# The last store of a scan-and-FFN kernel as two stores of 64 rows on two queues

## The chip, the cores and the metric

The kernel runs on one core of a Trainium2 chip. A core has five engines with their own instruction streams: TensorE (PE, matmuls, with its weight loads listed as PEld), VectorE (DVE), ScalarE (ACT), GpSimd (POOL) and SyncE (SP). SyncE does no arithmetic here; it issues almost all DMA transfers. A transfer is issued by an engine's instruction and then carried out by the core's 16 DMA engines; its landing is signalled by a semaphore. The metric is the device time of one execution in microseconds, as the median of several runs.

## The reference: what is computed

Input x has 2048 tokens of 512 numbers. It is normalised per token, and the normalised xn goes two ways that are multiplied at the end:

```python
xn = layernorm(x)
s  = 2 * Re(scan(xn) @ C.T) + xn * Dskip      # diagonal complex recurrence over the 2048 tokens, 512 states
g  = silu((gelu(xn @ w_gate) * (xn @ w_up)) @ w_down)      # 512 -> 1376 -> 512
out = x + s * g                                # bf16, 2048 x 512
```

## The kernel before

The 2048 tokens are worked on in four slabs (s = 0 to 3) of 512, each of four tiles (m = 0 to 3) of 128 tokens. For a slab the kernel normalises, turns the tokens by a transposing DMA, multiplies by gate and up weights (`gate_tile`, L436), turns the product (`at_t`, L463), multiplies by the down weights (`down_pair`, L471), and beside that runs the recurrence (`half`, L537), whose scans are on VectorE. The output of a tile is made in `y_part` (L488), called by `y_tile` (L515):

- ScalarE puts the skip term into a PSUM bank (L493), TensorE adds eight matmuls to it (L497);
- VectorE multiplies the bank by the gate g (L502) and adds x (L508) into an output buffer `ot[o]`;
- SyncE stores the buffer to `out` (L513), 128 rows, one row per token.

Tiles are 512 columns wide. The last tile of all (s = 3, m = 3) goes in two halves of 256 columns (`HD`), each with its own bank, multiply, add and store, so that the last store has 128 rows of 256 columns, 64 KB. For the tiles m = 0 and m = 1 of the last slab, `cuts` (L511) makes two stores of 256 columns out of the one buffer after its addition is done; all other stores are of 512 columns, 128 KB. The last two tiles use two buffers of their own, which the trace calls `junk`, so they wait for no earlier store.

Nothing is scheduled automatically. `Plan.add` collects steps with what they read and write, and `Plan.run` (L70) emits them in a list written out at the head of the file, `ORDER` (L21). Every engine executes its own instructions in the order in which they appear there. An instruction waits for the semaphores of what it reads; a DMA also waits until the transfer that used its semaphore before has landed. At the end of the program (L840 in the trace) SyncE waits for the transfers that are still out, and then all engines meet in a closing sequence.

ScalarE issues only three small DMAs, at the head of the kernel (L256, the parameters `pv`); all the others are on SyncE.

Of the kernel before, what the change touches and what calls it, by code (L numbers as in the profile page):

```python
# [17 lines left out]
PE, ACT, DVE, POOL, SP = "PE", "ACT", "DVE", "POOL", "SP"  # L18
# [26 lines left out]
)  # L45


# [33 lines left out]
def kernel(  # L81
# [17 lines left out]
    nc = tc.nc  # L99
    P = 128  # L100
    S = 2048
    D = 512
# [6 lines left out]
    NS = S // TS  # L109
    M = TS // P  # L110
# [4 lines left out]
    HD = D // 2  # L115
# [5 lines left out]
    V, A, G, T = nc.vector, nc.scalar, nc.gpsimd, nc.tensor  # L121
# [6 lines left out]
    def sb(name, shape, dt=BF16):  # L128
        return consts.tile(shape, dt, name=name)
# [30 lines left out]
    ot = [sb(f"ot{i}", [P, D]) for i in range(2)]  # L160
# [18 lines left out]
    def dve(n, emit, reads=(), writes=(), rate=1.0, base=DV, **kw):  # L179
        return pl.add(DVE, base + n / 960.0 / rate, emit, reads, writes, lag=0.13, **kw)  # L180

    def acts(n, emit, reads=(), writes=(), ptr=0, **kw):
        return pl.add(ACT, AC + 0.12 * ptr + n / 1200.0, emit, reads, writes, lag=0.16, **kw)

    def pe(n, cols, emit, reads=(), writes=(), **kw):
        return pl.add(PE, n * (cols + 6) / 2400.0, emit, reads, writes, lag=0.22, **kw)
# [4 lines left out]
    def dma(eng, issue, land, emit, reads=(), writes=(), **kw):  # L191
        return pl.add(eng, issue, emit, reads, writes, lag=land, **kw)
# [3 lines left out]
    out_td = out[0]  # L196
# [291 lines left out]
    def y_part(s, m, c0, c1, bank, key, seed, e):  # L488

        w = c1 - c0  # L490
        ps = bank[:, 0:w]
        if seed:
            acts(w, lambda: act(out=ps, in_=sk[s % 2][:, m, c0:c1], func=AF.Copy), [("sk", s % 2, m)], [key])  # L493

        def f():
            for j in range(2 * NPT):
                T.matmul(ps, lhsT=hst[s % 2][:, j // NPT, j % NPT, m * P : (m + 1) * P], rhs=C2[:, j // NPT, j % NPT, c0:c1],  # L497
                         start=(j == 0 and not seed), stop=(j == 2 * NPT - 1), skip_group_check=True)
        pe(2 * NPT, w, f, [("hst", s % 2, 0), ("hst", s % 2, 1)] + C2S + ([key] if seed else []), [key])
        gi, b = g2s[s, m]  # L500
        if seed:
            dve(w, lambda: V.tensor_tensor(out=yg[e][:, c0:c1], in0=ps, in1=g2[gi][:, b, c0:c1], op=ALU.mult), [key, ("g2", gi, b)], [("yg", e, c0)])  # L502
        else:
            ys = tF[:, 0, c0:c1]
            dve(w, lambda: V.tensor_tensor(out=ys, in0=ps, in1=sk[s % 2][:, m, c0:c1], op=ALU.add), [key, ("sk", s % 2, m)], [("tF",)])
            dve(w, lambda: V.tensor_tensor(out=yg[e][:, c0:c1], in0=ys, in1=g2[gi][:, b, c0:c1], op=ALU.mult), [("tF",), ("g2", gi, b)], [("yg", e, c0)])
        o = 2 + m % 2 if s == NS - 1 and m >= M - 2 else m % 2
        dve(w, lambda: V.tensor_tensor(out=ot[o][:, c0:c1], in0=yg[e][:, c0:c1], in1=x_tok[:, s * M + m, c0:c1], op=ALU.add),  # L508
            [("yg", e, c0), ("x", s, m)], [("ot", o, c0)], rate=2.0)
        mg = s * TS + m * P  # L510
        cuts = (0, HD) if (NS - 1, 0) <= (s, m) < (NS - 1, M - 2) else (c0,)  # L511
        for lo, hi in zip(cuts, (*cuts[1:], c1)):
            dma(SP, 0.35, 1.5, lambda lo=lo, hi=hi: nc.sync.dma_start(out=out_td[mg : mg + P, lo:hi], in_=ot[o][:, lo:hi]), [("ot", o, c0)], [("out", s, m, lo)], svc=(2, 0.4, 0.9))  # L513

    def y_tile(s, m):  # L515
        i = y_n[0] % 2
        seed = True
        y_n[0] += 1
        if (s, m) == (NS - 1, M - 1):
            for h in range(2):  # L520
                r, ps = bank()
                y_part(s, m, h * HD, (h + 1) * HD, ps, ("bank", r), True, m % 2)
        else:
            y_part(s, m, 0, D, ybank[i], ("y", i), seed, m % 2)
# [175 lines left out]
    c1, s1 = cbt[:, :, 1], sbt[:, :, 1]  # L700
# [32 lines left out]
    for pt in range(NPT):  # L733
# [3 lines left out]
            out=C2[:, 0, pt, :], in0=CT[:, 0, pt, :], scalar=cre[:, pt : pt + 1], in1=tF[:, 1, :], op0=ALU.mult, op1=ALU.subtract),  # L737
            ["coef", ("CT", 0), ("tF",)], [("C2", 0, pt)], base=0.13)
        dve(512, lambda pt=pt: V.scalar_tensor_tensor(
            out=C2[:, 1, pt, :], in0=CT[:, 1, pt, :], scalar=ncre[:, pt : pt + 1], in1=tF[:, 0, :], op0=ALU.mult, op1=ALU.subtract),  # L740
# [104 lines left out]
```

## Time and profile before

| | |
|---|---|
| median of 3 runs | 178.52 us (178.51 to 178.72) |
| span of the profiled execution, first to last instruction | 176.3 us |
| time around the span (median less span) | 2.2 us |
| PE busy | 172.3 us (98%) |
| DVE busy | 156.9 us (89%) |
| ACT busy | 123.5 us (70%) |
| last instruction that computes (DVE, L508) | starts at 173.60 us, takes 0.29 us |
| stores by SyncE | 19, of which 16 from `ot` and 3 from `junk` |

The profile is of one execution; its times are counted from the first instruction. The time of that execution as a run was not recorded apart from its span, so the span stands for it, with the 2.2 us around it. In the rows, "SPq" and "ACTq" are the instruction queues of SyncE and ScalarE that issue DMAs; the time of such a row is that of the issue, not of the transfer. "To landing" is from the issue to the last semaphore event of the transfer.

### The profile page before, as it was taken

What the parts mean: (1) busy time and instruction counts of PE and PEld (TensorE: products, weight loads), DVE (VectorE), ACT (ScalarE), POOL (GpSimd) and SP (SyncE); (2) the same over time, 40 slices, a digit from 0 to 9 for tenths busy, and PEclk for the clock granted to TensorE, in tenths of its full rate; (3) what the DMA queues carried; (4) which work ended last, traced back from release to release, by engine and by line L of the source; (5) the groups of instructions that cost most, each with busy time, mean ns of one, the idle gap of its engine ahead of it and who ended that gap; (6) DMA issues with size and microseconds to landing.
All of it is one profiled execution on the core that took longest, in us unless ns stands there. A gap on an engine that the chain in (4) does not pass through costs nothing.

```text
span 176.3 us, 2421 instructions
## 1 busy us (share of the span) xinstructions
PE 172.3 (98%) x847; PEld 82.3 (47%) x847; DVE 156.9 (89%) x252; ACT 123.5 (70%) x236; POOL 11.2 (6%) x25
## 2 busy tenths in 40 slices
PE   8999999999999999999999999999999999999992
PEld 2555454444454544444455454444444455444451
DVE  3859999999699984999979999899999999999764
ACT  6599979969999999799588845383058518482240
POOL 2660030000200000000040000000000000000000
PEclk9999999999999999999999999999999999999999
DMA  5999999998000809422000084194000007627112
GB/s 156 322 371 225 205 226 260 219 279 137 0 0 12 188 20 192 95 75 46 0 0 6 30 137 95 41 182 86 0 0 0 0 30 162 65 41 154 45 58 76
DMA packets 48355, 18.66 MB, mean 106 GB/s; under 512 B 40312, under 2 KB 47832, under 8 KB 48344
## 3 DMA queue, kind: packets, MB, share of 16 engines
q1 hardware_dynamic: 48320, 18.52, 48.8%
q8 instruction: 6, 0.10, 0.3%
q14 instruction: 5, 0.04, 0.1%
q10 hardware_dynamic: 24, 0.00, 0.0%
HBM read 6.46 MB, written 2.10 MB: 49 GB/s over the span
## 4 chain that ended last, share of the span: by engine, by line
PE 97%; DVE 1%; issue 0%; DVEq 0%
PE ring L449 32%; PE ring L481 22%; PE ring L547 16%; PE ybank L497 15%; PE ring L418 5%; PE ring L388 3%; PE ybank L418 2%; PE ring L299 1%; DVE yg L502 1%; PE ybank L299 1%; DVE junk L508 1%; PE ybank L328 0%; PE ring L303 0%; PE ring L313 0%; PE ring L603 0%
## 5 line engine op out<-in xcount | busy, mean ns | idle before, releaser
L449 PEld LDWEIGHTS <-xnT 128*128 128x128 bf16 x288 | 28.2, 98 | 28.4
L481 PE MATMUL ring<-wd,atT 128*128 128x512 bf16 (+1 forms) x176 | 39.3, 379 | 0.0
L449 PE MATMUL ring<-wg,xnT 128*128 128x512 bf16 (+1 forms) x144 | 31.6, 357 | 0.0
L449 PE MATMUL ring<-wu,xnT 128*128 128x512 bf16 (+1 forms) x144 | 31.3, 357 | 0.0
L547 PE MATMUL ring<-xnT,BT 128*128 128x512 bf16 x128 | 30.1, 379 | 0.0
L578 DVE TENSOR_TENSOR_SCAN Fs<-rho,ini,W 128x512 bf16<-128x512 f32 x24 | 29.7, 1271 | 0.1
L452 ACT ACTIVATE ub<-ring 128x512 bf16<-128x512 f32 (+1 forms) x36 | 19.2, 555 | 13.8 <-PE ring L449 13.7
L497 PE MATMUL ybank<-C,hst 128*128 128x512 bf16 x120 | 27.7, 379 | 0.0
L481 PEld LDWEIGHTS <-atT 128*128 128x128 bf16 (+1 forms) x176 | 17.2, 97 | 20.9
L549 ACT ACTIVATE U<-ring 128x512 bf16<-128x512 f32 x32 | 18.1, 599 | 7.5 <-PE ring L547 7.5
L452 ACT ACTIVATE gt<-ring 128x512 bf16<-128x512 f32 (+1 forms) x36 | 19.5, 556 | 3.7 <-PE ring L449 3.5
L497 PEld LDWEIGHTS <-hst 128*128 128x128 bf16 x136 | 13.3, 98 | 14.0
L484 ACT ACTIVATE g<-ring 128x512 f32<-128x512 f32 x16 | 9.4, 594 | 14.3 <-PE ring L481 14.2
L547 PEld LDWEIGHTS <-BT 128*128 128x128 bf16 x128 | 12.5, 97 | 14.8
L559 DVE TENSOR_TENSOR Q<-U,tab 128x4096 bf16<-128x4096 bf16 x8 | 18.3, 2289 | 0.9 <-ACT tab L646 0.7
L559 DVE TENSOR_TENSOR Q<-Fs,tab 128x4096 bf16<-128x4096 bf16 x8 | 18.3, 2288 | 0.1
L502 DVE TENSOR_TENSOR yg<-ybank,g 128x512 bf16<-128x512 f32 x15 | 10.2, 685 | 5.8 <-PE ybank L497 5.7
L763 ACT ACTIVATE junk<-x_tok 128x512 bf16<-128x512 bf16 x16 | 10.0, 632 | 1.2 <-DMA x_tok<-in_A_x_dram 1.2
L493 ACT ACTIVATE ybank<-sk 128x512 f32<-128x512 bf16 x15 | 9.1, 605 | 1.7 <-DVE yg L502 1.6
L768 ACT ACTIVATE xna<-x_tok,nb,rs 128x512 bf16<-128x512 bf16 x12 | 9.5, 812 | 0.0
L578 DVE TENSOR_TENSOR_SCAN Fs<-rho,W 128x512 bf16<-128x512 f32 x8 | 9.3, 1210 | 0.1
L458 DVE TENSOR_TENSOR at<-gt,ub 128x1024 bf16<-128x1024 bf16 x12 | 8.2, 683 | 0.0
(140 smaller groups left out, 169.7 us busy)
## 6 DMA issues: line engine op xcount, KB each, us to landing
x_tok<-in_A_x_dram SPq DMA_DIRECT2D x3, 512.0 KB, 4.6
out_dram<-ot SPq DMA_DIRECT2D x12, 128.0 KB, 1.8
wd<-in_B_w_down_dram SPq DMA_DIRECT2D x1, 1280.0 KB, 7.1
wu<-in_B_w_up_dram SPq DMA_DIRECT2D x4, 256.0 KB, 3.9
wg<-in_B_w_gate_dram SPq DMA_DIRECT2D x1, 864.0 KB
x_tok<-in_A_x_dram SPq DMA_DIRECT2D x4, 128.0 KB, 2.1
wg<-in_B_w_gate_dram SPq DMA_DIRECT2D x1, 512.0 KB, 6.0
wu<-in_B_w_up_dram SPq DMA_DIRECT2D x1, 352.0 KB, 5.3
```

Of the source, the lines that this page charges most:

```text
L418: T.matmul(ps[:, 0 : b - a], lhsT=lhs(k), rhs=wt[:, k, a:b], start=(k == 0), stop=(k == KT - 1))
L449: T.matmul(ps[:, 0 : b - a], lhsT=xnT[:, s % 2, m, k, :], rhs=wt[:, k, a:b], start=(k == 0), stop=(k == KT - 1))
L452: acts(b - a, lambda: act(out=dst[:, a:b], in_=ps[:, 0 : b - a], func=AF.Copy if up else AF.Gelu_apprx_tanh), [("bank", r)], [key], table= ...
L481: T.matmul(ps[:], lhsT=atT[:fs, k, m * P : (m + 1) * P], rhs=wd[:fs, k, :], start=(k == 0), stop=(k == NFT - 1))
L497: T.matmul(ps, lhsT=hst[s % 2][:, j // NPT, j % NPT, m * P : (m + 1) * P], rhs=C2[:, j // NPT, j % NPT, c0:c1], start=(j == 0 and not seed ...
L502: dve(w, lambda: V.tensor_tensor(out=yg[e][:, c0:c1], in0=ps, in1=g2[gi][:, b, c0:c1], op=ALU.mult), [key, ("g2", gi, b)], [("yg", e, c0)])
L547: T.matmul(ps[:], lhsT=BT[:, ri, k, pt * P : (pt + 1) * P], rhs=xnT[:, s % 2, :, k, :], start=(k == 0), stop=(k == KT - 1))
L549: acts(512, lambda q=q, ri=ri, ps=ps: act(out=U[ui][:, ri, q, :], in_=ps[:], func=AF.Copy), [("bank", r)], [("U", ui, q, ri)])
L559: dve(4096, lambda: V.tensor_tensor(out=Qf, in0=src.unsqueeze(1).to_broadcast(WQ), in1=table, op=ALU.mult), reads, ["Q"], rate=2.0)
L578: pl.add(DVE, 1.12 if s == 0 else 1.185, lambda ri=ri, q=q, pt=pt, first=first: V.tensor_tensor_scan(out=Fs[:, ri, q, :], data0=rho[:, pt ...
L763: acts(512, lambda i=i, fn=fn, sc=sc, m=m: act(out=junk()[:], in_=x_tok[:, s * M + m, :], func=fn, scale=sc, accum_out=sx[:, s, i, m : m + ...
L768: acts(512, lambda m=m: act(out=xn[m], in_=x_tok[:, s * M + m, :], func=AF.Identity, scale=rs[:, s, m : m + 1], bias=nb[:, s, m : m + 1]), ...
```

## The change

Two edits in `y_part`, and the list `ORDER` numbered anew for them. The second half of the last tile is stored by two DMAs of 64 rows each: rows 0 to 63 by SyncE, rows 64 to 127 by ScalarE. Both read the same buffer and wait for the same addition. And of the last slab only tile 0 is still stored in two halves of columns; tile 1 is stored whole. In `ORDER` the numbers shift by one for the step that falls away, and ScalarE's new DMA is step 671, the last step of ScalarE. On TensorE, VectorE and GpSimd the instructions and their order are the same in both kernels; SyncE has one store less in tile 1, and ScalarE one DMA more.

```diff
-    586, 639, 637, 640, 601, 641, 626, 635, 630, 616, 643, 646, 644, 651, 652, 638, 647, 657, 658, 642, 662, 663, 667, 668, 636, 631, 648, 653, 654,
-    659, 660, 664, 665, 669, 670, 649, 650, 655, 656, 661, 666, 671,
+    586, 639, 637, 640, 601, 641, 626, 635, 630, 616, 643, 646, 644, 651, 652, 638, 647, 656, 657, 642, 661, 662, 666, 667, 636, 631, 648, 653, 654,
+    658, 659, 663, 664, 668, 669, 671, 649, 650, 655, 660, 665, 670,
...
         mg = s * TS + m * P
-        cuts = (0, HD) if (NS - 1, 0) <= (s, m) < (NS - 1, M - 2) else (c0,)
+        if (s, m, c1) == (NS - 1, M - 1, D):
+            for eng, issue, p0 in ((SP, nc.sync, 0), (ACT, A, P // 2)):
+                dma(eng, 0.25, 1.4, lambda issue=issue, p0=p0: issue.dma_start(out=out_td[mg + p0 : mg + p0 + P // 2, c0:c1], in_=ot[o][p0 : p0 + P // 2, c0:c1]),
+                    [("ot", o, c0)], [("out", s, m, c0, p0)])
+            return
+        cuts = (0, HD) if (s, m) == (NS - 1, 0) else (c0,)
         for lo, hi in zip(cuts, (*cuts[1:], c1)):
             dma(SP, 0.35, 1.5, lambda lo=lo, hi=hi: nc.sync.dma_start(out=out_td[mg : mg + P, lo:hi], in_=ot[o][:, lo:hi]), [("ot", o, c0)], [("out", s, m, lo)], svc=(2, 0.4, 0.9))
```

## The prediction

> **What bounds the kernel now.** I read the chain of work that ended last first, then its tail in order of time, then what SyncE does behind it, then the transfers in the last two microseconds. On the page, the chain's shares by engine:
>
> ```profile
> PE 97%; DVE 1%; issue 0%; DVEq 0%
> ```
>
> TensorE carries 97% of the chain, and the change touches none of its instructions: the order of PE, VectorE (DVE) and GpSimd is the same in both kernels, and ScalarE (ACT) has one DMA more at its end. So only what stands behind the last matmul can move. The chain's end in order of time (start, length, what):
>
> ```profile
> 171.42 0.70 DVE yg L502
> ...
> 172.57 0.35 DVE yg L502
> ...
> 172.94 0.29 DVE junk L508
> 173.23 0.35 DVE yg L502
> ...
> 173.60 0.29 DVE junk L508
> ```
>
> The last instruction that computes ends at 173.60 + 0.29 = 173.89, but the page gives a span of 176.3. The remaining 2.4 us are the last store and the closing of the program, which the chain of work leaves out. The stores that SyncE issues in that stretch, one window of its timeline each:
>
> ```profile
> 170.80 0.33 SPq L513 DMA_DIRECT2D out_dram<-ot  x1
> 171.18 0.42 SPq L513 DMA_DIRECT2D out_dram<-ot  x1
> 172.59 0.33 SPq L513 DMA_DIRECT2D out_dram<-junk  x1
> 173.26 0.33 SPq L513 DMA_DIRECT2D out_dram<-junk  x1
> 173.91 0.33 SPq L513 DMA_DIRECT2D out_dram<-junk  x1
> ```
>
> The first two rows are the halves of tile 1 of the last slab, the third is tile 2 whole, the last two are the halves of tile 3. The very last store is issued at 173.91, 0.02 us after its addition ended. Next, what the DMA engines do from there on (one row for each stretch; the last two columns are their mean busy share and GB/s):
>
> ```profile
> 174.24:174.74 0.50, 0.00 (x0) 0.00 (x0) 0.00 (x0) 0.00 (x0) 0.00 (x0) 1.00 0.21 57
> 174.74:175.10 0.36, 0.00 (x0) 0.00 (x0) 0.00 (x0) 0.00 (x0) 0.00 (x0) 1.00 0.63 182
> 175.10:175.46 0.36, 0.00 (x0) 0.00 (x0) 0.00 (x0) 0.00 (x0) 0.00 (x0) 1.00 0.00 0
> 175.46:176.28 0.82, 0.00 (x0) 0.00 (x0) 0.00 (x0) 0.00 (x0) 0.00 (x0) 1.00 0.00 0
> ```
>
> The 64 KB of the last store move only in the second row, 0.36 us. Before it lie 0.33 us of issue and 0.50 us in which its packets have not begun (the 0.21 of the first row is the store before it); behind it 0.36 us with nothing on the engines before SyncE hears that the store landed. What SyncE waits for at the end, and when (waits from 172 on, longest first; then its closing waits at L840, by window):
>
> ```profile
> SPq L840 <- DMA out_dram<-junk: 0.9, 2, 0.6
> ...
> L840 SPq EVENT_SEMAPHORE  x3: 28/28/28, 174.4 to 174.5; - x3
> ...
> L840 SPq EVENT_SEMAPHORE  x2: 28/28/28, 174.5 to 174.8; - x2
> ...
> L840 SPq EVENT_SEMAPHORE  x1: 28/28/28, 175.5 to 175.5; - x1
> ```
>
> So the tail of before reads: addition ends 173.89; issue 173.91 to 174.24; first packets 174.74; last packets 175.10; landed and waited for at 175.46 (1.5 us after the issue); closing 0.82; end 176.28. This 1.55 us from the addition to the wait is all that the change can work on.
>
> I make the sum against that span. The median of the runs shown is 178.52, that is 2.2 us more than 176.3; those 2.2 us lie around the span, and I take them as unchanged.
>
> **Part 1: tile 1 of the last slab as one store.** Removed is one store instruction. Before, SyncE is done with the two halves at 171.18 + 0.42 = 171.60 and its next store can't go before the addition that ends at about 172.57 (its row is 172.59), so SyncE idles for 0.99 us. One whole store is issued in 0.33 at 170.80 (the 128 KB store at 172.59 took the same 0.33 as the 64 KB ones), so SyncE is free at 171.13 and waits longer for the same addition. Its landing (median time from issue to landing, by size):
>
> ```profile
> out_dram<-ot SPq DMA_DIRECT2D x12, 128.0 KB, 1.8
> ...
> out_dram<-ot SPq DMA_DIRECT2D x4, 64.0 KB, 1.6
> ...
> out_dram<-junk SPq DMA_DIRECT2D x2, 64.0 KB, 1.5
> ```
>
> At 1.8 it lands at 172.6 instead of 171.18 + 1.6 = 172.8. Nobody waits for either before SyncE's closing waits, which start at 174.3, and no later addition writes that buffer again. The next packets on the engines are those of the store at 172.59, whose own issue and lead of about 0.83 us put them at 173.4. Cost and gain: 0. The cover is the 0.99 us of idle SyncE; if it were gone, the second issue, 0.42, would count.
>
> **Part 2: the second half of tile 3 as two stores of 64 rows.** Both wait for the addition that ends at 173.89. SyncE's store sits where the old one sat. ScalarE's DMA stands behind its last activation and only the closing stands behind it; ScalarE is free long before: its last two instructions, from its timeline,
>
> ```profile
> 169.69 0.68 ACT L493 ACTIVATE ring<-sk 128x256 f32<-128x256 bf16 x2
> ```
>
> end at 170.37, so nothing of ScalarE is delayed, and the added wait has nobody behind it.
>
> Step by step, each against the old store:
>
> (a) SyncE's issue. The rows give 0.33 for 64 KB and for 128 KB of 128 rows, so bytes don't set it. No 64-row store is in the trace. The nearest with fewer rows are the three small loads at the head, four rows each, on ScalarE's queue:
>
> ```profile
> L256 ACTq DMA_DIRECT2D pv<-in_A_log_dt_dram x1: 554/554/554, 0.8 to 0.8; - x1
> L256 ACTq DMA_DIRECT2D pv<-in_A_Lambda_im_dram x1: 259/259/259, 1.4 to 1.4; - x1
> L256 ACTq DMA_DIRECT2D pv<-in_A_Lambda_re_dram x1: 314/314/314, 1.7 to 1.7; - x1
> ```
>
> Bounds: 0 to -0.07 (0.33 to 0.26). I take 0, since 64 rows are nearer to 128 than to 4 in what an engine gets. This is not yet a gain of the kernel, because ScalarE's half must land too.
>
> (b) ScalarE's issue. The same three rows: 0.26 to 0.55, against the old 0.33, so -0.07 to +0.22. The first, 0.55, came when this queue had issued nothing before and a table load was running on ScalarE; the later two took 0.26 and 0.31. At 173.9 the queue has been idle for 172 us, which speaks for the slow one; ScalarE is otherwise idle, which speaks for the fast ones. I take the middle row, 0.31, which is level with SyncE's 0.33: 0.
>
> (c) The packets. 64 KB in 0.36 us at a mean share of 0.63 over the core's 16 engines (the second of the four stretches): at least eleven of them take part in one store already. Two halves on the same engines are the same bytes; if they run side by side, the last packet ends when it ended before. If each half had its engines to itself, it would take half of 0.36, a gain of 0.18; if one half were started wholly behind the other, 0. A check by landing: 128 KB in 1.8, 64 KB in 1.5 to 1.6, so half the bytes would be worth 0.10 to 0.15 at most. Bounds 0 to -0.18; I take 0, since one store spreads over most engines now and the two halves overlap in time.
>
> The rule that speaks against this edit: the Trainium skill, "DMA: Bandwidth & Descriptors", section "Rules for kernel authors", says of two transfers to disjoint partition halves not to bother, since both spread over the same 16 engines, whichever engine issues them. By that rule (c) is 0; without it (c) would be up to -0.18. The trace agrees as far as it goes (share 0.63 as a mean over 16 engines with one store in flight), but no run yet shows two queues storing at once.
>
> (d) The closing. SyncE now waits for two last stores. In the rows above three closing waits that were due at once stand within 174.33 to 174.50, and each takes 28 ns: a pitch of about 0.06. If the half whose wait comes first in the list lands last, its partner's wait follows for 0.06 more; if it lands first, 0. I take 0.03.
>
> Sum: part 1 0, (a) 0, (b) 0, (c) 0, (d) +0.03: the span goes from 176.3 to 176.33, the time from 178.52 to 178.55. A measurement of this kernel can tell about 0.2%, that is 0.36 us, from no change; the forecast is that nothing can be told.
>
> **The rivals.**
>
> Rival 1, faster: the fixed parts shrink with the rows. If issue and the 0.50 us ahead of the first packet depend on how many rows a queue must describe, and the two queues do this side by side, then the issue falls by 0.07 (a), the packets by 0.18 (c), and some of the 0.50 goes as well; a quarter of it would be 0.13. Together -0.38, 178.14. For it: 0.83 of the 1.55 us lie before the first packet, and two engines would share that work. Against it: stores of 64 KB and 128 KB with the same 128 rows took the same 0.33, and a load of 4 rows still took 0.26, so nearly all of the issue stands whatever the rows. Half of this rival, -0.15 to -0.25, lies within 0.2%.
>
> Rival 2, slower: ScalarE's queue is cold. Place: ScalarE's one DMA at 173.9, the first on that queue since 1.7 us. Price: an issue like the first row, 0.55 instead of 0.33, +0.22; its wait comes after SyncE's half, +0.06; and a landing like the slower stores (1.6 where the last one takes 1.5), +0.10. Together +0.38, 178.90. It decides from the point where ScalarE's half lands later than 175.46, which is as soon as its issue takes longer than SyncE's with the same lead. For it: 172 us without a DMA on that queue. Against it: the 0.55 happened beside a table load and beside SyncE's first load, and its successors overlapped SyncE's issues at 0.26 and 0.31. With the issue alone, +0.22 or +0.28 with (d), the time would be 178.74 to 178.80, within 0.2%.
>
> Rival 3, the change doesn't do what it says: part 1 does nothing in any case (SyncE idles 0.99 us there), and part 2 leaves the same 1.5 us of issue, lead, packets and receipt, only twice. That is 178.52 and coincides with the forecast but for 0.03; it has no time of its own.
>
> **How the numbers follow.** Forecast with rival 3: 0.66, all within 0.2%. Rival 1: 0.16, of which 0.10 is faster by over 0.2% (below 178.16). Rival 2: 0.18, of which 0.14 is slower by over 0.2% (above 178.88; I give the full price most, because an idle queue can cost in its lead too, which no row bounds). So faster 0.10, within 0.2% 0.76, slower 0.14. The range: the unknown costs reach from -0.25 ((a) and (c)) to +0.38 (rival 2), which is 178.27 to 178.90; the runs of before lie between 178.51 and 178.72, and I add some 0.05 at either end for that, 178.20 to 178.95. Outside are left the full rival 1 and the worst of rival 2.
>
> **What would show it.** In the profile of the changed kernel: SyncE's last store starts 0.02 after the last addition and takes 0.33 or less (a); ScalarE's stands beside it with 0.26 to 0.55 (b); the last stretch of packets is still about 0.36 long (c) - if it is 0.2, rival 1 is right; the last closing wait stands about 1.55 us after the addition's end, and the closing behind it is still 0.82 (d). SyncE idles between 171.13 and 172.59 (part 1). The prediction is wrong if the distance from the last addition to the last closing wait differs from 1.55 by more than 0.25, or if the last addition itself no longer ends at 173.89: the second would mean that something other than the stores has moved, which I see no reason for.

## The result, and the profile after

| | before | changed | ratio (95% interval) |
|---|---|---|---|
| median of 6 runs | 178.59 us (178.43 to 178.72) | 179.44 us (179.28 to 179.76) | 1.0043 (1.0028 to 1.0059) |
| span of the profiled execution | 176.3 us | 177.8 us | |

The change made the kernel slower by 0.85 us between the medians; by the interval of the ratio it is 0.5 to 1.05 us. The forecast was 178.55, no change that can be told; the time lies above the range. Three later runs of over 180.9 us, in a slower state, are left out of the ratios and ranges below.

The two profiled executions differ by 1.5 us, more than the two medians do. All runs whose span was recorded have 1.7 to 1.9 us around it, not the 2.2 that median less span gave, so the profiled execution of before was itself a fast one, of about 178.1 us. The 1.5 us fall into two parts. The end of the last addition and the stores of the changed kernel, from the timelines of VectorE, SyncE and ScalarE (start, length, engine, line):

```profile
174.44 0.29 DVE L508 TENSOR_TENSOR junk<-yg,x_tok 128x256 bf16<-128x256 bf16 x1
```

```profile
171.65 0.33 SPq L518 DMA_DIRECT2D out_dram<-ot  x1
...
173.44 0.33 SPq L518 DMA_DIRECT2D out_dram<-junk  x1
...
174.10 0.33 SPq L518 DMA_DIRECT2D out_dram<-junk  x1
174.76 0.56 SPq L513 DMA_DIRECT2D out_dram<-junk  x1
```

```profile
174.76 0.56 ACTq L513 DMA_DIRECT2D out_dram<-junk  x1
```

The last addition ends at 174.73 instead of 173.89, so 0.84 us of the 1.5 lie ahead of the last stores, which part 2 changes; where they come from is told at the end. From there to the end of the span it was 176.28 - 173.89 = 2.39 us and is 177.78 - 174.73 = 3.05 us: 0.66 us more, and that is the change. Below, this distance is called the tail; it frees the comparison from what happened earlier in an execution.

Both of the 64-row stores start 0.03 us after the addition (the forecast had 0.02), but both issues take 0.56 us where each 128-row store above them takes 0.33. The tail by stretches, in the view that gave the four stretches of before (length, busy times of the engines, granted clock, DMA share, GB/s):

```profile
174.76:175.32 0.56, 0.00 (x0) 0.00 (x0) 0.00 (x0) 0.00 (x0) 0.00 (x0) 1.00 0.40 117
175.32:175.96 0.64, 0.00 (x0) 0.00 (x0) 0.00 (x0) 0.00 (x0) 0.00 (x0) 1.00 0.00 0
175.96:176.53 0.57, 0.00 (x0) 0.00 (x0) 0.00 (x0) 0.00 (x0) 0.00 (x0) 1.00 0.48 115
176.53:176.96 0.43, 0.00 (x0) 0.00 (x0) 0.00 (x0) 0.00 (x0) 0.00 (x0) 0.97 0.00 0
176.96:177.78 0.82, 0.00 (x0) 0.00 (x0) 0.00 (x0) 0.00 (x0) 0.00 (x0) 0.50 0.00 0
```

Against before: issue 0.56 for 0.33 (+0.23), the wait for the first packet 0.64 for 0.50 (+0.14), the packets 0.57 for 0.36 (+0.21), receipt and closing waits 0.43 for 0.36 (+0.07), closing 0.82 as before. Sum +0.65. The third stretch, cut where the queues change over, shows the packets by queue (q1 is SyncE's, q10 ScalarE's; packets, MB, share; first 175.96 to 176.23, then 176.23 to 176.53):

```profile
q1 hardware_dynamic: 79, 0.03, 50.1%
...
q10 hardware_dynamic: 80, 0.03, 46.9%
q1 hardware_dynamic: 1, 0.00, 0.2%
```

Each half has 80 packets, 64 of a row and 16 small ones; the 128-row store has the same 16 beside its 128 rows. The halves do not run side by side: ScalarE's begins when all of SyncE's packets but one small one have begun. Cut there, they take 0.27 and 0.30 one after the other, where 128 rows at once took 0.36. That two halves of the partitions serialize is what the Trainium skill, "DMA: Bandwidth & Descriptors", section "Rules for kernel authors", states; by that rule alone the packets would cost nothing. It describes the packets of two queues as interleaved; here those of the two halves are not.

### The profile page after: what moved, and what is told of

It reads as the page before. It is cut to its first block, busy times and chain, and to the rows that moved or that the text cites. A ratio compares the mean times of both kernels' runs of the same rounds, so it can differ in the third digit from the quotient of the medians.

```text
span 177.8 us, 2406 instructions
## 1 busy us (share of the span) xinstructions
PE 172.3 (97%) x831; PEld 82.8 (47%) x847; DVE 157.0 (88%) x252; ACT 123.6 (70%) x236; POOL 11.4 (6%) x25
## 4 chain that ended last, share of the span: by engine, by line
PE 96%; DVE 1%; issue 1%; DVEq 0%
PE ring L449 31%; PE ring L481 21%; PE ring L552 16%; PE ybank L497 14%; PE ring L418 5%; PE ring L388 3%; PE ybank L418 2%; PE ring L299 1%; DVE yg L502 1%; PE ybank L299 1%; DVE junk L508 1%; PE ybank L328 0%; PE ring L313 0%; PE ring L303 0%; PE ring L608 0%
```

## The experiments

The first theory, formed from the rows above, was that two queues that issue at the same moment slow each other, since both show 0.56. The rivals: a store of 64 rows is dear by itself; ScalarE's queue is cold after 172 us; or the loss lies in part 1 or in the head.

**e1: part 1 alone.** The split is left out.

```diff
-        cuts = (0, HD) if (NS - 1, 0) <= (s, m) < (NS - 1, M - 2) else (c0,)
+        cuts = (0, HD) if (s, m) == (NS - 1, 0) else (c0,)
```

> Part 1 alone: tile 1 of the last slab stored whole, the last store as before. My theory (the loss is made by two queues issuing at the same moment) says that this part costs nothing: ratio to the kernel before 1.000 within 0.002, and from the end of the last addition to the end of the span 2.39 us as before (3.05 in the changed kernel). The rival that the whole store of tile 1 is in the way of the later stores gives part of the 0.85 us here.

Measured: 178.63 against 178.63 us, ratio 1.0006 (0.9989 to 1.0023). Its last addition starts at 173.78 and takes 0.29, its span is 176.51: a tail of 2.44. Part 1 costs nothing that the time can tell. The 0.05 by which the tail is longer is one closing wait that stands behind the wait on the last store here and not in the kernel before; e8 comes back to it.

**e2: part 2 alone.** The split of the changed kernel, with the old `cuts`.

> Part 2 alone: the last store split by rows over the two queues, tile 1 still in halves. Every theory that puts the loss behind the last addition expects all of it here: 3.05 us from the end of the last addition to the end of the span, issues of 0.56 on both queues, ratio 1.003 to 1.005. If the ratio stays at 1.000, the loss came from part 1 or from the head of the kernel.

Measured: ratio 1.0037 (1.0019 to 1.0055), which is 0.66 us of 178.6: the size of the difference of the tails. Both issues again:

```profile
174.46 0.56 SPq L513 DMA_DIRECT2D out_dram<-junk  x1
...
174.47 0.56 ACTq L513 DMA_DIRECT2D out_dram<-junk  x1
```

The split makes the loss. The tail is 177.42 - 174.44 = 2.98, a little less than the 3.05 expected: in the changed kernel one closing wait stands behind the wait on ScalarE's half, here none does.

**e3: both halves on SyncE.**

```diff
-            for eng, issue, p0 in ((SP, nc.sync, 0), (ACT, A, P // 2)):
+            for eng, issue, p0 in ((SP, nc.sync, 0), (SP, nc.sync, P // 2)):
```

> Both 64-row stores on SyncE's queue, one behind the other; ScalarE issues nothing. Theory (two queues at the same moment): the first issue takes 0.33 as a 128-row store does, the second 0.33 to 0.43 as in the back-to-back pairs of before, and the end is 0.2 to 0.4 us later than before because of the second issue. Rival (a store of 64 rows is dear by itself): the first issue takes 0.56 here too. Rival (ScalarE's queue is cold): 0.33 and 0.43, like the theory.

Measured: ratio 1.0062 (1.0041 to 1.0083). The two issues and their landing:

```profile
L513 SPq DMA_DIRECT2D out_dram<-junk x2: 558/568/577, 174.5 to 175.1; - x2
...
DMA to landing us min/median/max: 1.8/1.8/1.8
```

With ScalarE out of it the first issue still takes 558 ns. The first theory falls here; "64 rows are dear" was right. The second issue takes 577 ns, right behind the first, so this is worse than the changed kernel: a tail of 177.79 - 174.43 = 3.36.

**e4: the last store whole on ScalarE.**

```diff
-            for eng, issue, p0 in ((SP, nc.sync, 0), (ACT, A, P // 2)):
-                dma(eng, ...
+            dma(ACT, 0.35, 1.5, lambda: A.dma_start(out=out_td[mg : mg + P, c0:c1], in_=ot[o][:, c0:c1]), [("ot", o, c0)], [("out", s, m, c0)])
```

> The last store whole, 128 rows, on ScalarE's queue alone; SyncE issues nothing then. Theory (two queues at the same moment): issue 0.33, first packet 0.83 behind its start, span and time as before, ratio 1.000 within 0.002. Rival (ScalarE's queue is cold after 172 us): issue 0.55 and the end 0.2 us or more later, ratio 1.001 to 1.003.

Measured: ratio 1.0007 (0.9993 to 1.0022).

```profile
174.26 0.38 ACTq L512 DMA_DIRECT2D out_dram<-junk  x1
```

The issue takes 0.38, 0.05 more than on SyncE, and the tail is 176.7 - 174.23 = 2.5. A queue that was idle for 172 us is not cold in any way that counts. What made the kernel's first parameter load take 0.55 is open; 172 us of idleness alone do not cost that.

**e5: half of the store left out.** Rows 0 to 63 on SyncE as in the changed kernel; rows 64 to 127 of this piece aren't stored.

```diff
-            for eng, issue, p0 in ((SP, nc.sync, 0), (ACT, A, P // 2)):
+            for eng, issue, p0 in ((SP, nc.sync, 0),):
```

> Rows 0 to 63 of the last store on SyncE as in the changed kernel; the store of rows 64 to 127 is left out, so 64 rows of 256 columns of the output are not written. It takes the second queue away and leaves the 64-row store. The theory that stands now (a store of 64 rows is dear by itself: issue 0.56, first packet 1.20 behind its start) says that half the bytes take longer than the whole 128 rows: 2.7 us from the end of the last addition to the end of the span, against 2.39 before and 3.05 in the changed kernel; time 1.001 to 1.003 of before. What is left to 3.05, about 0.3, is then the price of the second queue beside it. The rival (two queues at the same moment) says 2.3 to 2.4.

Measured: ratio 1.0029 (1.0013 to 1.0045). From its timeline and its stretches:

```profile
174.94 0.56 SPq L513 DMA_DIRECT2D out_dram<-junk  x1
```

```profile
174.94:176.14 1.20, 0.00 (x0) 0.00 (x0) 0.00 (x0) 0.00 (x0) 0.00 (x0) 1.00 0.19 55
176.14:176.44 0.30, 0.00 (x0) 0.00 (x0) 0.00 (x0) 0.00 (x0) 0.00 (x0) 1.00 0.45 108
```

Half the bytes take longer than the whole: 1.20 us from the issue to the first packet against 0.83, and packets of 0.30, not of half of 0.36. The tail is 177.66 - 174.91 = 2.75, 0.36 more than before. The other 0.30 up to 3.05 is what the second half on its queue adds.

**e6: split by columns instead of rows**, 128 rows of 128 columns on each queue.

```diff
+            ch = (c1 - c0) // 2
+            for eng, issue, q0 in ((SP, nc.sync, c0), (ACT, A, c0 + ch)):
+                dma(eng, 0.25, 1.4, lambda issue=issue, q0=q0: issue.dma_start(out=out_td[mg : mg + P, q0 : q0 + ch], in_=ot[o][:, q0 : q0 + ch]), ...
```

> The last store split by columns: all 128 rows, 128 columns on SyncE's queue and 128 on ScalarE's, at the same moment. If the count of rows makes the issue dear, both issues take 0.33 to 0.38 here and the first packet stands 0.83 to 0.9 behind them; the end is then 0.1 to 0.4 us later than before for the packets alone, which are twice as many (256 instead of 128, 256 bytes each). If two queues at the same moment make it dear, both issues take 0.56 and the end is 0.6 us later or more.

Measured: ratio 1.0013 (0.9997 to 1.0030).

```profile
174.87 0.33 SPq L514 DMA_DIRECT2D out_dram<-junk  x1
...
174.87 0.38 ACTq L514 DMA_DIRECT2D out_dram<-junk  x1
```

```profile
174.87:175.70 0.83, 0.00 (x0) 0.00 (x0) 0.00 (x0) 0.00 (x0) 0.00 (x0) 1.00 0.28 79
175.70:176.11 0.41, 0.00 (x0) 0.00 (x0) 0.00 (x0) 0.00 (x0) 0.00 (x0) 1.00 0.72 160
```

Two queues at the same moment issue at their usual 0.33 and 0.38 with the usual lead of 0.83. Twice the packets take 0.41, so at 128 rows the queues do overlap in part. The tail is 177.39 - 174.84 = 2.55: still 0.16 more than with one store, though the ratio's interval doesn't exclude 1.

**e7 and e9: other row counts, away from the end.** Earlier stores of 512 columns are split by rows on SyncE's queue; the last store is as before, and each of the two ran once. The first store of each group is read. From e7; e9 has other rows in the same place:

```diff
+            rows = {(0, 0): (0, 32, P), (0, 2): (0, 64, P), (1, 0): (0, 16, P), (1, 2): (0, 96, P), (NS - 1, 1): (0, 64, P)}.get((s, m), (0, P))
...
+                for p0, p1 in zip(rows, rows[1:]):
+                    nc.sync.dma_start(out=out_td[mg + p0 : mg + p1, lo:hi], in_=ot[o][p0:p1, lo:hi])
```

> A probe away from the end: five earlier stores of 128 rows by 512 columns are split by rows on SyncE's queue into 32 and 96, 64 and 64, 16 and 112, 96 and 32, and 64 and 64 rows; the last store is as before. Read are the issue and the lead to the first packet of the first of each pair. If it is the count of rows under 128 that is dear, all of them take about 0.56 and 1.2; if it goes with the bytes, the 64-row stores of 512 columns (64 KB like the last store of before) take 0.33; if it grows with the rows up to 64, 16 rows are cheapest and 96 dearer than 64.

> A second probe away from the end, stores of 512 columns on SyncE's queue, read at the first of each group: 48, 80, 112 and 56 rows, and 64 rows that begin at row 32 instead of row 0. If 64 rows are a case of their own, 48, 80 and 112 take 0.31 to 0.36 with a lead of 0.81 to 0.86 like 16, 32, 96 and 128, and 64 rows from row 32 take 0.56 and 1.20 again. If the row at which they begin decides, the store from row 32 takes 0.33. 56 rows are the nearest count to 64 that is no multiple of 16.

The issues (ns; one window each), first e7 with 32, 64, 16, 96, 128 (of 256 columns) and 64 rows, then e9 with 48, 64 from row 32, 80, 112 and 56:

```profile
L517 SPq DMA_DIRECT2D out_dram<-ot x1: 352/352/352, 74.3 to 74.3; - x1
...
L517 SPq DMA_DIRECT2D out_dram<-ot x1: 557/557/557, 100.2 to 100.2; - x1
...
L517 SPq DMA_DIRECT2D out_dram<-ot x1: 342/342/342, 113.2 to 113.2; - x1
...
L517 SPq DMA_DIRECT2D out_dram<-ot x1: 317/317/317, 141.5 to 141.5; - x1
...
L517 SPq DMA_DIRECT2D out_dram<-ot x1: 333/333/333, 169.7 to 169.7; - x1
...
L517 SPq DMA_DIRECT2D out_dram<-ot x1: 505/505/505, 171.3 to 171.3; - x1
```

```profile
L518 SPq DMA_DIRECT2D out_dram<-ot x1: 357/357/357, 74.4 to 74.4; - x1
...
L518 SPq DMA_DIRECT2D out_dram<-ot x1: 622/622/622, 100.3 to 100.3; - x1
...
L518 SPq DMA_DIRECT2D out_dram<-ot x1: 317/317/317, 113.3 to 113.3; - x1
...
L518 SPq DMA_DIRECT2D out_dram<-ot x1: 316/316/316, 141.6 to 141.6; - x1
...
L518 SPq DMA_DIRECT2D out_dram<-ot x1: 394/394/394, 171.4 to 171.4; - x1
```

The lead from the issue's start to the first packet, from the packet records of the same traces: 0.81 to 0.86 us for 16, 32, 48, 56, 80, 96, 112 and 128 rows, and 1.20, 1.16 and 1.27 for the three stores of 64. It is not "fewer rows than 128", nor the bytes (64 rows of 512 columns are the same 64 KB as the last store of before), nor the row at which they begin. Of the nine counts tried, 64 alone is dear. 56 and 80 are the nearest ones read in this way; other counts between them are open.

Two other things also make an issue dear in these traces, which is why only the first store of a group, with hardly a packet in flight, is read. Behind a 64-row store the next issue is dear too: in e9 the 32 rows right behind the 64 took 0.73. So the second issue of e3 proves nothing about its own count. And a 128-row store issued at 104.0 in e7, while the packets of a transposing DMA were in flight, took 1.02.

**e8: 96 rows on SyncE, 32 on ScalarE.**

```diff
-            for eng, issue, p0 in ((SP, nc.sync, 0), (ACT, A, P // 2)):
+            for eng, issue, p0, p1 in ((SP, nc.sync, 0, 96), (ACT, A, 96, P)):
```

> The changed kernel with one number altered: the last store split by rows as 96 on SyncE and 32 on ScalarE instead of 64 and 64, at the same moment. The probe showed 0.32 and 0.35 for the issue of 96 and 32 rows against 0.56 for 64. If 64 rows are what is dear, both issues are 0.31 to 0.38, the first packet stands 0.82 behind, the packets of both take 0.36 to 0.45 together, and from the end of the last addition to the end of the span it is 2.4 to 2.55 us (2.39 before, 3.05 in the changed kernel): ratio to before 1.000 to 1.001. If two queues storing rows side by side are dear whatever their count, it stays near 3.05 and 1.003 or more.

Measured: ratio 1.0024 (1.0003 to 1.0044).

```profile
174.34 0.34 SPq L513 DMA_DIRECT2D out_dram<-junk  x1
...
174.34 0.38 ACTq L513 DMA_DIRECT2D out_dram<-junk  x1
```

```profile
174.34:175.17 0.83, 0.00 (x0) 0.00 (x0) 0.00 (x0) 0.00 (x0) 0.00 (x0) 1.00 0.27 79
175.17:175.62 0.45, 0.00 (x0) 0.00 (x0) 0.00 (x0) 0.00 (x0) 0.00 (x0) 1.00 0.61 146
175.62:176.18 0.56, 0.00 (x0) 0.00 (x0) 0.00 (x0) 0.00 (x0) 0.00 (x0) 1.00 0.00 0
```

Issue and lead are back at 0.34 and 0.83, as expected. The tail is 176.97 - 174.31 = 2.66, more than the 2.4 to 2.55 expected and less than 3.05: packets +0.09, and receipt with the closing waits 0.56 instead of 0.36. Other than with 64 and 64 rows, the packets of the two queues overlap here (from 175.35 to 175.55):

```profile
q1 hardware_dynamic: 57, 0.02, 46.5%
q10 hardware_dynamic: 39, 0.01, 25.6%
```

How much of a tail belongs to the last store shows in the closing waits. SyncE makes them one after another, about 0.06 us apart when they are due at once, and the wait on the last store needn't be the last of them. e7 and e9 end with the same 128-row store as before, and so does e1; in all four the wait on its landing starts 1.57 us after the last addition. But one further wait stands behind it in e1, three in e9 and four in e7, and the tails are 2.44, 2.58 and 2.64 instead of 2.39. From e7, the wait on the last landing and the four behind it:

```profile
L845 SPq EVENT_SEMAPHORE  x5: 28/28/28, 176.0 to 176.2; - x5
```

So the fairer measure is the time from the end of the last addition to the start of the wait on the last landing:

| last store | run | us |
|---|---|---|
| 128 rows on SyncE | before, e1, e7, e9 | 1.57 in each |
| 128 rows on ScalarE | e4 | 1.62 |
| two halves by columns, two queues | e6 | 1.67 |
| 96 and 32 rows, two queues | e8 | 1.78 |
| 64 rows on SyncE, the rest left out | e5 | 1.88 |
| 64 and 64 rows, two queues | changed, e2 | 2.16, 2.17 |
| 64 and 64 rows, both on SyncE | e3 | 2.53 |

Of the 0.66 us of the change, 0.59 is this later landing and 0.06 the one closing wait behind it. Of the 0.59, 0.38 go when 64 and 64 rows become 96 and 32, and 0.21 stay: 0.09 in the packets and 0.12 in the receipt, whose cause is open. No other split by rows was tried. The times of whole runs can't tell e8 from e2, 1.0024 against 1.0037 with intervals that overlap; the traces can. No version with two queues came out ahead of one 128-row store; the kernel before stands.

## Why the prediction was wrong, point by point

- **What bounds the kernel, and how the tail of before divides:** right, but for 1.55 us from the addition to the wait, which is 1.57 (1.55 is from the issue). The start of the issue (0.03 after the addition) and the closing (0.82) came as forecast.
- **What would show it:** both signs of being wrong came. From the last addition to the last closing wait it is 176.95 - 174.73 = 2.22 instead of 1.55. And the last addition no longer ended at 173.89; that is the head of this execution, not the change.
- **Part 1, 0:** right for the stores and within what the time can tell (e1). The sum didn't have that a changed count of stores also changes which closing wait comes last, 0.05 in e1.
- **(a) SyncE's issue, 0 with bounds 0 to -0.07:** this step failed, and with it the forecast. It measured +0.23, and the wait between issue and first packet, which had no term of its own but as a gain in rival 1, another +0.14. The step put 64 rows between 4 and 128 (by count they are no nearer to 128 than to 4) and took it that the cost lies between theirs; e7 and e9 show that it doesn't. No row of before showed a 64-row store, and bounds from neighbours on both sides were no bounds.
- **(b) ScalarE's issue, 0:** 0.56 instead of 0.31, probably for the same cause: e4 has 0.38 for 128 rows on that queue, e8 0.38 for 32. No run has 64 rows on ScalarE without 64 on SyncE beside them.
- **(c) the packets, 0 with bounds 0 to -0.18:** outside the bounds, +0.21. The step allowed for both orders, side by side and one wholly behind the other, and priced either at 0. The halves ran one behind the other; what failed is that half the rows were to take half of 0.36. 64 rows alone need 0.30 (e5).
- **(d) the closing, +0.03:** receipt and closing waits together +0.07, of which 0.06 is the partner's wait: the wait on ScalarE's half comes first in the list and that half lands last, as the step allowed.
- **Rival 1** was wrong in its premise: the fixed part grew at 64 rows, and at the eight other counts it didn't shrink (issue 0.32 to 0.39, lead 0.81 to 0.86). **Rival 2** had the right sign and half of the place, but the wrong mechanism: e4 excludes the cold queue, and SyncE's issue was as dear as ScalarE's. That its 0.55, read off a load of four rows, met the 0.56 is luck. Its 178.90 was too low because the lead and the packets grew too, by 0.14 and 0.21.
- **Noise:** I took 0.2% from three runs within 0.21 us. In the later sets the same kernel before ran from 178.04 to 179.75 us, so a range of 178.20 to 178.95 was too narrow even for it.

Why 64 rows in particular are dear is open: the runs show which counts are, not what the issuing engine does differently. Only stores were tried, not loads. That ScalarE's half follows SyncE's is seen in the packets of 64 and 64 rows, while in e6 and e8 the two queues' packets overlap; what holds ScalarE's half back was not tried.

## What to carry to other kernels

A store that ends the program costs mostly what doesn't go with its bytes: here 0.83 us before its first packet and 0.36 behind its last, of 1.55 from the issue. Cutting it in two made neither of these shorter in any run here, and no cut shortened the 0.36 of packets in between; the cut into 96 and 32 rows over two queues cost 0.27 us in its trace though both issues were cheap. A changed count of stores also changes which closing wait comes last, at 0.06 us for each wait behind the last landing. And the cost of an issue needn't lie between those of its neighbours: look for the very shape in a trace, or measure it away from the critical path as e7 did, before bounding it.

## What the runs showed of the hardware that I had not expected

**64 rows.** On SyncE, an issue of 0.51 to 0.62 us and a lead of 1.16 to 1.27, at 256 and 512 columns, from row 0 or 32, against 0.32 to 0.39 and 0.81 to 0.86 for eight other counts from 16 to 128. On ScalarE the issue of 64 rows was 0.56 against 0.38 for 32 and 128; its lead with nothing beside it was not measured.

**The last landing is steady.** With the same last store, its wait started 1.57 us after the last addition in four executions of four kernels; what differed between their tails was the place of that wait among the closing waits.

**The head varies.** The 0.84 us ahead of the last addition come from the first 7 us, where both kernels execute the same instructions. TensorE's groups there (mean ns of one before the bar), before from 3.5 to 7 us, and then changed from 3.5 to 7.5:

```profile
L388 PE MATMUL ring<-wu,W 128*128 128x512 bf16 x9 | 2.3, 378 | 0.0
L328 PE MATMUL ybank<-ident,xna 128*128 128x128 bf16 x8 | 0.8, 220 | 0.0
```

```profile
L388 PE MATMUL ring<-wu,W 128*128 128x512 bf16 x7 | 2.2, 444 | 0.0
L328 PE MATMUL ybank<-ident,xna 128*128 128x128 bf16 x8 | 1.0, 265 | 0.0
```

The same matmuls are slower at first in the changed kernel's execution. From the timelines, matmuls of 512 columns, before and then changed (the first row is the same in both):

```profile
1.57 2.34 PE L299 MATMUL ring<-const-bfloat16-1.0 128*128 128x512 bf16 x5
...
5.00 0.59 PE L388 MATMUL ring<-wu,W 128*128 128x512 bf16 x2
...
5.65 1.67 PE L388 MATMUL ring<-wu,W 128*128 128x512 bf16 x7
```

```profile
5.42 1.00 PE L388 MATMUL ring<-wu,W 128*128 128x512 bf16 x2
...
6.49 0.81 PE L388 MATMUL ring<-wu,W 128*128 128x512 bf16 x3
```

At first such matmuls start about 0.43 us apart (L299 at 1.57, 2.00, 2.42), later 0.22 apart (the seven of L388 at 5.65, 5.86, 6.08). Before, the first two of L388 already run at the fast pace; in the changed kernel's execution they start 0.40 apart, and the fast pace is there from 6.49 on. From that row on the same matmuls start 0.84 us later than before (6.49 for 5.65). The column of the granted clock says 1.00 for all of this, but the traces' own records of the clock begin only at 4.04 us before and at 6.27 us in the changed kernel, and the column counts what stands ahead of them as 1.00. A part of the 0.84 can also come from the load of x: ScalarE's L347, which waits for it, starts at 3.58 instead of 3.33. How the two share is not known.

The Trainium skill, "TensorE: Matmul & The Clock Gate", section "Part 1: The HAM clock gate (the "warmup" mystery)", says that TensorE runs at half rate until a free-running activity window of about 3.4 us has found it busy. The half rate agrees with 0.43 for 0.22. A window that starts at a different moment in each execution would fit the different moments of the change, and the spread of the runs; that is argued, not shown.

The head is why the tails, and ratios over many runs, carry the verdicts here, and not the two spans.
